# One PSUM bank per head, matmuls ordered by array shape, and GpSimd held behind VectorE in an attention and gated-MLP kernel

## The chip, the cores and the metric

The kernel runs on one core of a Trainium2 chip. The metric is the device time of one execution in microseconds (us), median of the runs shown; lower is better.

## What is computed

Eight batch entries, 12 heads, 448 positions, head size 64. Attention with RMS-normed q and k, then a gated MLP with a residual:

```python
q_n, k_n = (rmsnorm(q, g_q), rmsnorm(k, g_k))
scores = matmul(q_n, k_n.T) / sqrt(64)
attn = exp(scores - max); attn = attn / (sum(attn) + 1e-09)
x = heads side by side of matmul(attn, v)          # (8, 448, 768)
h = gelu_tanh(x @ w_in)                            # w_in (768, 1024)
u, v = h[..., :512], h[..., 512:]
v_n = (v - mean) / sqrt(var + 1e-06) * g_ln
v_s = einsum('ts,bsd->btd', w_sg, v_n) + b_sg      # over positions
out = x + (u * v_s) @ w_out                        # w_out (512, 768)
```

All inputs and the output are float32 (some inputs are handed to the device as 64-bit words and decoded there); most matmuls run on pairs of float16 parts, high and low.

## The kernel before

The kernel does not issue instructions as it is written. `tile_attn_gmlp_kernel` records every operation on a `Tape`, as tasks with a priority (its place in the program plus an offset). `Tape.schedule` then plays a list scheduler: each engine takes the ready task of lowest priority, each operation has a cost from `Tape.cost`, and START gives the delay between engines. `Tape.emit` issues everything in the planned order through one line (L425 of the profile), so nearly all rows of the profile carry this line and are told apart by their tiles. The engines run their queues in order, so the plan fixes what stands behind what.

The work is cut into 24 units of four heads. For each unit: squares and norms of q and k (`squares`, `norms`), the multiplications and the split into float16 halves (`split`: tiles qk and hl; by GpSimd, with VectorE and ScalarE), a transposing DMA into qt, then `scores`. There seven blocks t each give a pair of heads: 12 matmuls (tile s, in the 64x64 array shape, four at a time), on VectorE a minimum (tile jk, result nm), on ScalarE the exponential (tile ex), then its two halves (ahl) and a transposing DMA into at. `pv` makes the attention output in two parts per unit, 48 in all: the reciprocals of the sums in small steps on GpSimd and VectorE (rx, ry, rh, rl in `recips`), a factor row by TensorE (tile row, 128x64 shape), then 48 matmuls into tile pv. Of these 12 have 64 rows of contraction (64x64 shape) and 36 have 128 (128x64 shape). `moe` is the MLP of one batch entry: mv and mu (x @ w_in), a cluster of gelus, layernorm, ms (over positions), mo (residual and output), all but some of it in the 128x128 shape. `weights` decodes and splits the weights on VectorE and ScalarE (tiles dec, wi, wp, wr) during the first batches. MOFF is the offset that lets `moe` stand behind attention in priority.

A change of the array shape costs the planner SWITCH (133 or 92 ns), and it may put off a task of another shape while one of the present shape lies within HYST of it.

PSUM has eight banks. Before, four are a ring of two score tiles (pool ps_s, each tile both heads' banks), and four are given out by the plan to pv, row, psc and the MLP (pool ps_m, BANKS = 4, MOST: at most one pv tile and four of the MLP).

VectorE operations of some forms and all GpSimd operations are marked `port`: in the plan they do not overlap. Nothing enforces this when the kernel runs.

Of the kernel before, what the change touches and what calls it, by code (L numbers as in the profile page):

```python
# [24 lines left out]

MOFF, MOFF0, GP = 340, 100, 350

# [15 lines left out]

NS, BANKS, MOST = 2, 4, dict(pv=1, mm=4, mme=3)
NQK, NVR, RAWB = 2, 2, 3
# [7 lines left out]
BIAS = dict(A=0, V=0, G=0)  # L53
SLACK = (0, 0)
OVER, PATIENCE = dict(V=130, G=150), 300
START = dict(T=60, A=34, V=33, G=85, S=28, N=0)


class Tile:

    def __init__(self, pool, args, kw, tag, cap):
        self.pool, self.args, self.kw, self.tag, self.cap = pool, args, kw, tag, cap
        self.users, self.writes, self.reads, self.real, self.bank = [], [], [], None, None

# [32 lines left out]
class Tape:  # L97

    def __init__(self, tc):
        self.tc, self.tiles, self.tasks, self.off, self.count = tc, {}, [], 0, 0  # L100
        self.after = set()
        self.grouped = self.last = None
        self.masks, self.swap = {}, None

    def free(self, ap):
# [21 lines left out]
    def cost(self, q, op, a, kw):  # L127

        aps = [x for x in kw.values() if isinstance(x, bass.AP)]
        n = max([self.free(x) for x in aps], default=1)  # L130
        wide = [k for k in ("in_", "in0", "in1") if k in kw and self.free(kw[k]) > max(n // 2, 1)]
        psum = any(self.tiles[kw[k].tensor.name].pool.space for k in wide if kw[k].tensor.name in self.tiles)
        if q.eng == "T":
            t, big = kw["lhsT"], kw["rhs"]
            rows, cols = (64 if ap_n <= 64 else 128 for ap_n in (t.shape[0], self.free(t)))
            m = self.free(big)
            d = max(m / 2.4, 26.7 if cols == 64 else 53)
            if big.dtype == F32R:
                d = max(d, 186)
            if big.dtype == F32:  # L140
                d = max(4 * m / 2.4, 250)
            return d * rows * cols / 128 ** 2 + (4 if rows == cols == 128 else 3), 170, (rows, cols)
        if q.eng != "S" and "dma" in op:
            return 700, 4000, None
        if q.eng == "S":
            b = n * kw["out"].shape[0] * mybir.dt.size(kw["out"].dtype)
            if "transpose" in op:
                return 1530, b / 458752, True
            return 600, b / 220e3, False
        if "preload" in op:  # L150
            return 1283, 0, None
        if q.eng == "A":
            ptr = sum(isinstance(kw.get(k), bass.AP) for k in ("bias", "scale"))
            return 0.833 * n + (70 if psum else 100) + 80 * ptr + (200 if "accum_out" in kw else 0), 100, None
        if q.eng == "V":
            if op == "reciprocal":
                return 70 + 6.5 * n, 75, None
            ptr = sum(isinstance(kw.get(k), bass.AP) for k in ("scalar", "scalar1", "scalar2"))
            one = len(wide) == 1 and not psum and "reduce" not in op and "bn" not in op
            f32 = one and (mybir.dt.size(kw[wide[0]].dtype) == 4 or kw[wide[0]].dtype == U16)  # L160
            return (0.52 if f32 else 1.04) * n + 75 + 40 * ptr + (70 if "accum_out" in kw else 0), 75, None
        if n < 100:
            return 1.5 * n + 185, 20, None
        wide = [k for k in wide if len([x for x in kw[k].ap if x[0]]) == len(kw[k].ap)]
        return (1.86 if len(wide) > 1 else 2.5 if op == "tensor_scalar" else 1.64) * n + 210, 20, None

    def port(self, q, op, kw):

        if q.eng == "G":
            return True  # L170
        if q.eng != "V" or max(self.free(v) for v in kw.values() if isinstance(v, bass.AP)) < 16 or op not in ("tensor_tensor", "scalar_tensor_tensor", "tensor_scalar", "tensor_copy"):
# [21 lines left out]
    def record(self, q, op, a, kw):  # L193
# [5 lines left out]
        pe = q.eng == "T"  # L199
        if t is None or self.grouped is None and not (pe and t.eng == "T" and t.key == (outs[0].tensor.name, mode)  # L200
                                                      and t.off == self.off):
            t = Task(q.eng, self.count + self.off)
            t.id, t.off, t.key = len(self.tasks), self.off, (outs[0].tensor.name, mode) if pe else None
            self.tasks.append(t)
# [42 lines left out]
    def schedule(self):  # L247
# [16 lines left out]
        for tl in self.tiles.values():  # L264
            if not tl.users:
                continue
            if tl.pool.name == "ps_m":
                kind = tl.kw["tag"]
                free_order = tl.kw["name"] in ("psc", "sw_")
                tl.users[0].opens.append((tl, kind, None if free_order else last.get(kind[:2])))  # L270
                if not free_order:
# [35 lines left out]
        while left:  # L307
            moved = True
            let_go()
            while moved:  # L310
                moved = False
                for e in START:
# [71 lines left out]
                    for s in succ[t.id]:  # L384
                        f = T[s].eng
                        r = free[e] + 15 if f == e and not T[s].alts else end + START[f]
                        ready[s] = max(ready[s], r)
# [15 lines left out]
    def emit(self, real_pools):  # L403
        tc = self.tc

        def real(v):
# [8 lines left out]
            return bass.AP(tensor=r.tensor, offset=v.offset, ap=v.ap)  # L415

        for t in self.schedule():
            for c in t.calls:
# [5 lines left out]
                first = (kw.pop("out"),) if op == "memset" else ()  # L424
                getattr(q.nc_eng, op)(*first, *a, **kw)  # L425


@with_exitstack
def kernel(
# [39 lines left out]
    for n_, b_, s_ in (("const", 1, None), ("ld", 3, None), ("prep", 2, None), ("att", 2, None), ("sml", 4, None),  # L469
                       ("xp", NX, None), ("ps_s", NS, PS), ("ps_m", 1, PS)):  # L470
# [3 lines left out]
    const, ld, prep, att, sml, xp, ps_s, ps_m = made  # L474
    mlp = Pool(tape, "mlp", 1)
# [86 lines left out]
    def decode(dst, raw, most=None):  # L562
# [3 lines left out]
        V.tensor_scalar(out=di, in0=hi, scalar1=0x7FFFFFFF, scalar2=None, op0=ALU.bitwise_and)  # L566
        if most is None:
            V.tensor_scalar(out=dst, in0=dst, scalar1=LEAST, scalar2=None, op0=ALU.max)
        else:
            V.tensor_scalar(out=dst, in0=dst, scalar1=LEAST, scalar2=None, op0=ALU.max, op1=ALU.max, accum_out=most)  # L570
        V.tensor_scalar(out=di, in0=di, scalar1=3, scalar2=0x3FFFFFF8, op0=ALU.logical_shift_left, op1=ALU.bitwise_and)
# [221 lines left out]
    def scores(u):  # L793
# [5 lines left out]
        for t in range(C7):  # L799
            if t in (0, C4):  # L800
                at = att.tile([P, 2 * C7, (C4 - t // C4) * P], F16, name=f"at{t // C4}", bufs=1)
                U[u]["at"].append(at)
            ps = ps_s.tile([P, 2, 512], F32, name="s")
            for m, (qx, kx) in enumerate(((0, 2), (1, 2), (0, 3))):
                for h in range(2):
                    hs = slice(h * HP, (h + 1) * HP)
                    for j in range(NG):
                        mm(out=ps[j * HP:(j + 1) * HP, h, 0:S].rearrange("p (c n) -> p c n", n=HP),
                           lhsT=qt[hs, qx, t * P + j * HP:t * P + (j + 1) * HP],
                           rhs=kt[hs, kx, j], start=(m == 0), stop=(m == 2))  # L810
            nm = sml.tile([P, 2], F32, name="nm", bufs=6)
            for h in range(2):
                jk = att.tile([P, S], BF16, name="jk", bufs=2)
                V.tensor_scalar(out=jk, in0=ps[:, h, 0:S], scalar1=UP, scalar2=None, op0=ALU.add, op1=ALU.min,
                                accum_out=nm[:, h:h + 1])
            ex = att.tile([P, 2, S], I32, name="ex", bufs=NEX)
            for h in range(2):
                A.activation(out=ex[:, h], in_=ps[:, h, 0:S], func=AF.Exp, scale=-1.0, bias=nm[:, h:h + 1], accum_out=sums[:, t, h:h + 1])
            yield
# [35 lines left out]
    def pv(u, e):  # L855
# [259 lines left out]
    pend = None  # L1115
    wts = low(weights(), 0)
    load_qk(0, [SP, A] if EARLY else None)
# [116 lines left out]
```

## Time and profile before

| | |
|---|---|
| median of three runs | 884.81 us (882.46 to 885.58) |
| the profiled execution | 881.78 us, of which the span of instructions is 880.0 |
| TensorE busy | 766.3 us, 87% of the span |
| ScalarE busy | 727.9 us, 83% |
| VectorE busy | 685.8 us, 78% |
| GpSimd busy | 317.6 us, 36% |
| mean granted TensorE clock | 0.957 |

Engines are PE (TensorE), PEld (its weight loads), DVE (VectorE), ACT (ScalarE), POOL (GpSimd) and SP (which starts DMAs). The busy share of TensorE is a mean over stages that differ; matmul ends are modelled, so times between starts say more than durations. Times in the rows are us from the span's start.

### The profile page before, as it was taken

To read this page: it belongs to the slowest core of one execution; us is meant where nothing else is said; L and a number is where in the kernel's file an instruction comes from. 1 tells how busy PE (TensorE), PEld (TensorE's weight loads), DVE (VectorE), ACT (ScalarE), POOL (GpSimd) and SP (SyncE) were. 2 spreads that over 40 slices of the span, in tenths; PEclk is the share of its full clock that TensorE was granted. 3 is DMA by queue.
4 is the path that set the end of the run, shared out by engine and by line. 5 is a ranking of instruction groups with operands and counts; after the bars stand their busy time and mean duration, and the time that the engine had idled before them with its cause. 6 is when DMAs were issued, how large, how long until landed. Compare 5 with 4: busy or idle time off the path is not lost.

```text
span 880.0 us, 20978 instructions
## 1 busy us (share of the span) xinstructions
PE 766.3 (87%) x7766; PEld 456.0 (52%) x7766; DVE 685.8 (78%) x1690; ACT 727.9 (83%) x1495; POOL 317.6 (36%) x458
## 2 busy tenths in 40 slices
PE   0445669547999999999999999999999999999997
PEld 0222334223574467544754477456745575457457
DVE  6899997998887987868877979688887978583150
ACT  4779789987988998989999989799999978884351
POOL 3554520274453344535433506542553341000000
PEclk9997869856999999999999999999999999999999
DMA  6999989889899959998999599969999698635002
GB/s 161 262 256 233 227 178 216 162 187 215 167 221 227 204 116 217 231 199 167 188 221 219 129 215 188 226 157 180 210 226 175 124 183 178 147 85 100 19 1 72
DMA packets 433942, 155.96 MB, mean 177 GB/s; under 512 B 402544, under 2 KB 427696, under 8 KB 433840
## 3 DMA queue, kind: packets, MB, share of 16 engines
q1 hardware_dynamic: 433840, 154.63, 85.8%
q8 instruction: 61, 1.00, 0.5%
q14 instruction: 41, 0.34, 0.1%
HBM read 43.57 MB, written 11.01 MB: 62 GB/s over the span
## 4 chain that ended last, share of the span: by engine, by line
PE 56%; DVE 18%; ACT 14%; issue 5%; DMA 3%; POOL 2%; SPq 0%; ACTq 0%; DVEq 0%; POOLq 0%
PE pv L425 11%; PE s L425 8%; DVE jk L425 4%; ACT ex L425 3%; DVE dec L425 3%; ACT ahl L425 3%; ACT L425 2%; PE row L425 2%; DMA at<-ahl 2%; DVE vl L425 1%; DVE ahl L425 1%; DVE ss L425 1%; ACT u L425 1%; POOL qk L425 1%; ACT sqk L425 1%
## 5 line engine op out<-in xcount | busy, mean ns | idle before, releaser
L425 ACT ACTIVATE ex<-s,nm 128x448 int32<-128x448 f32 x336 | 212.3, 634 | 29.8 <-DVE jk L425 25.3
L425 DVE TENSOR_SCALAR_CACHE_REDUCE jk<-s 128x448 bf16<-128x448 f32 x336 | 199.5, 617 | 43.5 <-PE s L425 42.6
L425 PE MATMUL s<-qt 64*64 64x448 f16 x2016 | 148.3, 383 | 79.7 <-ACT ex L425 58.1
L425 ACT ACTIVATE ahl<-ex 128x896 f16<-128x896 uint16 x191 | 179.7, 952 | 8.5 <-DMA at<-ahl 7.8
L425 PEld LDWEIGHTS <-vh 128*64 128x64 f16 (+2 forms) x1792 | 100.5, 111 | 89.7 <-issue 64.0
L425 PE MATMUL pv<-at,vh 128*64 128x256 f16 (+3 forms) x1536 | 140.8, 274 | 5.7 <-DMA at<-ahl 3.1
L425 PEld LDWEIGHTS <-qt 64*64 64x64 f16 x2016 | 62.5, 111 | 117.9 <-issue 76.7
L425 DVE TENSOR_SCALAR ahl<-ex 128x896 f16<-128x896 uint16 x145 | 103.7, 716 | 25.0 <-ACT ex L425 20.7
L425 POOL TENSOR_TENSOR hl<-qk,hl 128x896 f16<-128x896 f32 (+2 forms) x69 | 97.2, 1419 | 21.1 <-DVE hl L425 13.4
L425 POOL TENSOR_SCALAR rx<-sums 128x8 f32<-128x8 f32 (+1 forms) x48 | 16.5, 344 | 213.6 <-ACT ex L425 212.2
L425 POOL TENSOR_TENSOR qk<-qk,ny 128x896 f32<-128x896 f32 x47 | 83.1, 1787 | 1.8
L425 PEld LDWEIGHTS <-wi 128*128 128x128 f16 x576 | 52.0, 98 | 53.0 <-issue 7.7
L425 PE MATMUL pv<-at,vl 128*64 128x192 f16 (+3 forms) x768 | 74.4, 274 | 0.0
L425 PEld LDWEIGHTS <-vl 128*64 128x64 f16 (+2 forms) x896 | 49.3, 110 | 45.0 <-issue 27.7
L425 PEld LDWEIGHTS <-xh 128*128 128x128 f16 (+1 forms) x648 | 48.8, 103 | 42.9 <-issue 18.8
L425 POOL TENSOR_TENSOR qk<-qk,gg 128x896 f32<-128x896 f32 x23 | 48.4, 2106 | 60.3 <-ACT sqk L425 57.2
L425 ACT ACTIVATION_READ_ACCUMULATOR ex<-s,nm 128x1 f32 x336 | 69.0, 205 | 0.0
L425 DVE TENSOR_TENSOR pv<-pv,row 128x512 f32<-128x512 f32 (+1 forms) x48 | 30.2, 629 | 39.5 <-PE pv L425 39.3
L425 DVE TENSOR_REDUCE ss<-sqk 128x14 f32<-128x896 f32 x48 | 51.7, 1079 | 9.2 <-ACT sqk L425 9.1
L425 ACT ACTIVATE sqk<-qk 128x896 f32<-128x896 f32 x48 | 45.7, 954 | 2.9 <-DMA qk<-in_k_dram 1.5
L425 PEld LDWEIGHTS <-xl 128*128 128x128 f16 (+1 forms) x408 | 36.6, 103 | 20.4 <-issue 1.7
L425 ACT ACT_TABLE_LOAD x36 | 46.2, 1283 | 0.6
(1104 smaller groups left out, 1797.7 us busy)
## 6 DMA issues: line engine op xcount, KB each, us to landing
qk<-in_q_dram SPq DMA_DIRECT2D x48, 224.0 KB, 3.8
qk<-in_k_dram SPq DMA_DIRECT2D x48, 224.0 KB, 4.6
out_dram<-ot SPq DMA_DIRECT2D x56, 192.0 KB, 3.2
raw<-in_moe_w_in_dram SPq DMA_DIRECT2D x12, 512.0 KB, 5.3
vr<-in_v_dram SPq DMA_DIRECT2D x32, 192.0 KB, 3.6
vr<-in_v_dram SPq DMA_DIRECT2D x32, 144.0 KB, 3.6
rawo<-in_moe_w_out_dram SPq DMA_DIRECT2D x8, 384.0 KB, 4.0
at<-ahl SPq DMA_TRANSPOSE x168, 4.2
```

Of the source, the lines that this page charges most:

```text
L425: getattr(q.nc_eng, op)(*first, *a, **kw)
```

## The change

Four things change together.

- All eight PSUM banks go to pool ps_m and are given out by the plan. A score block has a tile, and so a bank, for each head. `mate` makes both heads' matmuls one task. `opens` lets a task start when as many banks are free as it needs and the kind's limit (MOST: pv 2, MLP 4, scores 6) allows it.
- `pv` goes through its matmuls by shape: the six 64-row blocks of both head pairs first, then the 128-row blocks, with cuts after blocks 5 and 14 (CUTS).
- `emit` adds a wait: a GpSimd operation marked `port` with a cost over LONG (500) waits for the last VectorE operation marked `port` that the plan put before it.
- The costs in `Tape.cost` are altered by some tens of ns, operations with accum_out are no longer marked `port`, MOFF goes from 340 to 300. WOFF = 0, AGAIN (15, and 85 for GpSimd) is new for a task that follows on its own engine.

```diff
-MOFF, MOFF0, GP = 340, 100, 350
+MOFF, MOFF0, GP = 300, 100, 350
-NS, BANKS, MOST = 2, 4, dict(pv=1, mm=4, mme=3)
+BANKS, MOST = 8, dict(pv=2, mm=4, mme=3, sc=6)
+LONG = 500
+CUTS = (5,14)
+AGAIN = dict(T=15, A=15, V=15, G=AG, S=15, N=15)
...
+        key = (self.tiles[outs[0].tensor.name].mate or outs[0].tensor.name, mode) if pe else None
...
         def opens(t, now):
-            return all((before is None or before.bank is not None) and min(bank_free) <= now
-                       and (held["pv"] if kind == "pv" else held["mm"] + held["mme"]) < MOST[kind]
-                       for _, kind, before in t.opens)
+            n = len(t.opens)
+            kind = t.opens[0][1] if n else None
+            return not n or (all(x is None or x.bank is not None for _, _, x in t.opens)
+                             and sum(x <= now for x in bank_free) >= n
+                             and (held["mm"] + held["mme"] if kind[:2] == "mm" else held[kind]) + n <= MOST[kind])
...
-                getattr(q.nc_eng, op)(*first, *a, **kw)
+                ins = getattr(q.nc_eng, op)(*first, *a, **kw)
+                if t.port and q.eng == "V":
+                    holder = ins
+                elif t.port and holder is not None and t.occ > LONG:
+                    tc.add_manual_dep(ins.ins, holder.ins.name, self.behind, reason="shared port")
...
-            ps = ps_s.tile([P, 2, 512], F32, name="s")
+            ps = [ps_m.tile([P, 512], F32, name="s", tag="sc") for h in range(2)]
+            for x in ps:
+                tape.tiles[x.tensor.name].mate = ps[0].tensor.name
...
-        for j in range(NG):
-            r = R[NG * u + j]
-            for k_, (v_, o, hx) in enumerate(blocks):
-                for h, (ks, c) in enumerate(hx):
-                    mm(out=pc[h * HP:(h + 1) * HP, j], lhsT=r[v_][ks, c], rhs=av[ks, o + c, j, 0:n],
-                       start=(j == 0 and k_ == 0), stop=(j == NG - 1 and k_ == len(blocks) - 1), skip_group_check=True)
-                if k_ == 5:
-                    yield
-            if j == 0:
+        steps = [(j, x) for part in (blocks[:3], blocks[3:]) for j in range(NG) for x in part]
+        for k_, (j, (v_, o, hx)) in enumerate(steps):
+            for h, (ks, c) in enumerate(hx):
+                mm(out=pc[h * HP:(h + 1) * HP, j], lhsT=R[NG * u + j][v_][ks, c], rhs=av[ks, o + c, j, 0:n],
+                   start=(k_ == 0), stop=(k_ == len(steps) - 1), skip_group_check=True)
+            if k_ in CUTS:
                 yield
```

In the order of TensorE's instructions the first place is one attention-output tile in the middle of the run. Before, this is the end of its first run of six in the 64x64 shape (vh and vl are the halves of v of one head pair, at1 the transposed exponentials, mu the MLP, wi its weight):

```order
L425 LDWEIGHTS vl_6449
L425 MATMUL pv_7276<-at1_6907,vl_6449 64x3x64
L425 LDWEIGHTS vh_6425
L425 MATMUL pv_7276<-at1_6907,vh_6425 64x3x64
L425 LDWEIGHTS vh_6425
L425 MATMUL pv_7276<-at1_6907,vh_6425 64x3x64
L425 LDWEIGHTS wi_779
L425 MATMUL mu__7263<-xh_6016,wi_779 128x448
```

It goes on in further runs of 6, 12, 6, 6 and 12 matmuls, with six of mu between (and a single other one, before the last), six runs in all. In the change the same kind of tile has the second head pair's blocks (vh_6647, vl_6677) straight behind the first's:

```order
L439 LDWEIGHTS vh_6548
L439 MATMUL pv_7272<-at1_7033,vh_6548 64x3x64
L439 LDWEIGHTS vh_6647
L439 MATMUL pv_7272<-at1_7033,vh_6647 64x3x64
L439 LDWEIGHTS vh_6647
L439 MATMUL pv_7272<-at1_7033,vh_6647 64x3x64
L439 LDWEIGHTS vl_6677
L439 MATMUL pv_7272<-at1_7033,vl_6677 64x3x64
```

Its runs are now 12, 18 and 18: three in place of six. Counted over the whole order, the array shape changes 606 times before and 363 times in the change; behind the first 1542 matmuls it is 485 and 280.

The second place is GpSimd's queue, at one unit's split, with the semaphores that each instruction waits for (DVE is VectorE's). Before:

```order
L425 TENSOR_TENSOR qk<-qk,ny 128x896 [waits DMAHW7_49,DMAHW0_49,Pool_49]
L425 TENSOR_TENSOR qk<-qk,ny 128x896
L425 TENSOR_TENSOR hl<-qk,hl 128x2x7x64 [waits DMAHW0_49,Activation_49]
L425 TENSOR_TENSOR hl<-qk,hl 128x2x4x64 [waits DMAHW6_49,Activation_49]
L425 TENSOR_TENSOR hl<-qk,hl 128x2x3x64 [waits Activation_49]
```

In the change:

```order
L439 TENSOR_TENSOR qk<-qk,ny 128x896 [waits DMAHW0_49,DMAHW7_49,DVE_49,Pool_49]
L439 TENSOR_TENSOR qk<-qk,ny 128x896 [waits DVE_49]
L439 TENSOR_TENSOR hl<-qk,hl 128x2x7x64 [waits DMAHW6_49,Activation_49]
L439 TENSOR_TENSOR hl<-qk,hl 128x2x4x64 [waits DMAHW0_49,DVE_49,Activation_49]
L439 TENSOR_TENSOR hl<-qk,hl 128x2x3x64 [waits DVE_49,Activation_49]
```

The operations and their order are the same; four of the five now wait for VectorE. Over the whole queue, 31 of 139 such long operations waited for VectorE before, and 98 of 138 do in the change. Beside this, one multiply (qk), one scaling (ahl) and one cast (hl) are on another engine than before.

## Rows read from the trace of the kernel before

**Rows 1.** Busy time in stretches: length, PE, PEld, DVE, ACT, POOL (instructions), clock, DMA.

```profile
0.00:50.00 50.00, 10.95 (x102) 5.55 (x103) 38.81 (x81) 29.41 (x55) 21.78 (x38) 1.00 0.91 213
50.00:100.00 50.00, 32.28 (x354) 17.07 (x353) 48.62 (x111) 44.64 (x90) 23.80 (x26) 0.86 1.12 244
100.00:150.00 50.00, 36.62 (x393) 19.69 (x390) 45.39 (x132) 42.84 (x85) 12.44 (x19) 0.80 1.01 195
150.00:200.00 50.00, 27.94 (x275) 15.04 (x274) 45.87 (x107) 46.57 (x98) 22.12 (x34) 0.74 0.87 187
200.00:250.00 50.00, 44.00 (x418) 27.12 (x421) 43.88 (x101) 43.61 (x88) 20.54 (x25) 0.85 0.99 192
250.00:300.00 50.00, 50.00 (x554) 27.29 (x554) 42.90 (x100) 43.37 (x94) 26.65 (x40) 1.00 1.08 223
...
400.00:500.00 100.00, 97.60 (x1004) 56.23 (x998) 82.83 (x201) 93.16 (x193) 47.95 (x63) 1.00 0.90 185
...
600.00:700.00 100.00, 97.88 (x1040) 57.08 (x1038) 83.27 (x205) 93.54 (x199) 41.49 (x59) 1.00 0.96 189
```

**Rows 2.** Waits of TensorE from 0 to 250 us: total us, times, longest.

```profile
PE s L425 <- ACT ex L425: 53.4, 21, 7.9
```

**Rows 3.** Waits of TensorE from 200 to 870 us.

```profile
PE s L425 <- ACT ex L425: 7.0, 9, 1.4
```

**Rows 4.** TensorE in order of time, 428 to 433 us: start, us, operation, shape, count.

```profile
428.46 0.52 PE L425 MATMUL pv<-at,vh 128*64 128x256 f16 x6
428.91 0.44 PE L425 MATMUL mo__6402<-wo_h,gh 128*128 128x384 f32 x1
429.19 0.34 PE L425 MATMUL mo__6402<-wo_l,gh 128*128 128x384 f32 x1
...
431.17 0.34 PE L425 MATMUL mo__6476<-wo_l,gh 128*128 128x384 f32 x1
431.34 0.34 PE L425 MATMUL mo__6476<-wo_h,gl 128*128 128x384 f32 x1
431.61 0.52 PE L425 MATMUL pv<-at,vl 128*64 128x256 f16 x6
431.96 0.49 PE L425 MATMUL pv<-at,vh 128*64 128x256 f16 x6
432.38 0.76 PE L425 MATMUL s<-qt 64*64 64x448 f16 x12
```

**Rows 5.** The chain that ended last, 80 to 120 us: start, us, what.

```profile
83.91 1.06 DVE hsv L425
...
86.82 2.26 DVE dec L425
...
97.23 2.13 DVE dec L425
...
113.33 1.77 DVE wi_up L425
```

**Rows 6.** VectorE in order of time, 84 to 104 us.

```profile
86.37 0.41 DVE L425 TENSOR_SCALAR dec<-dec 128x512 int32<-128x512 int32 x1
86.82 2.26 DVE L425 SCALAR_TENSOR_TENSOR dec<-raw,dec 128x512 int32<-128x512 int32 x1
...
97.15 2.22 DVE L425 TENSOR_SCALAR dec<-dec 128x512 int32<-128x512 int32 x1
...
100.83 0.68 DVE L425 SCALAR_TENSOR_TENSOR dec<-raw,dec 128x512 int32<-128x512 int32 x1
```

**Rows 7.** GpSimd in order of time, 84 to 104 us.

```profile
86.53 3.57 POOL L425 TENSOR_TENSOR hl<-qk,hl 128x896 f16<-128x896 f32 x2 [1.57 <-ACT hl L425]
...
97.00 2.08 POOL L425 TENSOR_TENSOR qk<-qk,gg 128x896 f32<-128x896 f32 x1 [2.67 <-ACT sqk L425]
```

**Rows 8.** Waits over the whole run: total us, times, longest.

```profile
POOL rx L425 <- ACT ex L425: 212.2, 31, 16.4
...
POOL hl L425 <- DVE hl L425: 13.4, 15, 1.8
...
PEld L425 <- POOL rh L425: 5.6, 5, 1.9
```

More of the change, by code (lines that the diff above doesn't have):

```diff
@@ L54 @@
 SLACK = (0, 0)
+LONG = 500
+WOFF = 0
+CUTS = (5,14)
+CA = 200
+CV = 70
+AG = 85
 OVER, PATIENCE = dict(V=130, G=150), 300
 START = dict(T=60, A=34, V=33, G=85, S=28, N=0)
+AGAIN = dict(T=15, A=15, V=15, G=AG, S=15, N=15)
 class Tile:
@@ L62, in __init__ @@
         self.pool, self.args, self.kw, self.tag, self.cap = pool, args, kw, tag, cap
-        self.users, self.writes, self.reads, self.real, self.bank = [], [], [], None, None
+        self.users, self.writes, self.reads, self.real, self.bank, self.mate = [], [], [], None, None, None
 class Pool:
@@ L103, in __init__ @@
         self.masks, self.swap = {}, None
+        self.behind = mybir.DependencyInfo(mybir.DependencyClass.Sync, mybir.DependencyReason.SCHED_ONLY)
     def free(self, ap):
@@ L153, in cost @@
             ptr = sum(isinstance(kw.get(k), bass.AP) for k in ("bias", "scale"))
-            return 0.833 * n + (70 if psum else 100) + 80 * ptr + (200 if "accum_out" in kw else 0), 100, None
+            return 0.833 * n + (52 if psum else 95) + 85 * ptr + (CA if "accum_out" in kw else 0), 100, None
         if q.eng == "V":
@@ L158, in cost @@
             ptr = sum(isinstance(kw.get(k), bass.AP) for k in ("scalar", "scalar1", "scalar2"))
-            one = len(wide) == 1 and not psum and "reduce" not in op and "bn" not in op
+            one = len(wide) == 1 and not psum and "reduce" not in op and "bn" not in op and "accum_out" not in kw
             f32 = one and (mybir.dt.size(kw[wide[0]].dtype) == 4 or kw[wide[0]].dtype == U16)
-            return (0.52 if f32 else 1.04) * n + 75 + 40 * ptr + (70 if "accum_out" in kw else 0), 75, None
+            return (0.52 if f32 else 1.04) * n + 70 + 50 * ptr + (CV if "accum_out" in kw else 0), 85, None
         if n < 100:
@@ L170, in port @@
             return True
-        if q.eng != "V" or max(self.free(v) for v in kw.values() if isinstance(v, bass.AP)) < 16 or op not in ("tensor_tensor", "scalar_tensor_tensor", "tensor_scalar", "tensor_copy"):
+        if q.eng != "V" or "accum_out" in kw or max(self.free(v) for v in kw.values() if isinstance(v, bass.AP)) < 16 or op not in ("tensor_tensor", "scalar_tensor_tensor", "tensor_scalar", "tensor_copy"):
             return False
@@ L199, in record @@
         pe = q.eng == "T"
-        if t is None or self.grouped is None and not (pe and t.eng == "T" and t.key == (outs[0].tensor.name, mode)
-                                                      and t.off == self.off):
+        key = (self.tiles[outs[0].tensor.name].mate or outs[0].tensor.name, mode) if pe else None
+        if t is None or self.grouped is None and not (pe and t.eng == "T" and t.key == key and t.off == self.off):
             t = Task(q.eng, self.count + self.off)
-            t.id, t.off, t.key = len(self.tasks), self.off, (outs[0].tensor.name, mode) if pe else None
+            t.id, t.off, t.key = len(self.tasks), self.off, key
             self.tasks.append(t)
@@ L269, in schedule @@
                 free_order = tl.kw["name"] in ("psc", "sw_")
-                tl.users[0].opens.append((tl, kind, None if free_order else last.get(kind[:2])))
+                before = last.get(kind[:2])
+                if free_order or any(x is before for x, _, _ in tl.users[0].opens):
+                    before = None
+                tl.users[0].opens.append((tl, kind, before))
                 if not free_order:
@@ L385, in schedule @@
                         f = T[s].eng
-                        r = free[e] + 15 if f == e and not T[s].alts else end + START[f]
+                        r = free[e] + AGAIN[e] if f == e and not T[s].alts else end + START[f]
                         ready[s] = max(ready[s], r)
@@ L566, in decode @@
         V.tensor_scalar(out=di, in0=hi, scalar1=0x7FFFFFFF, scalar2=None, op0=ALU.bitwise_and)
[L567 to L570, printed above, removed]
+        more = {} if most is None else dict(op1=ALU.max, accum_out=most)
+        V.tensor_scalar(out=dst, in0=dst, scalar1=LEAST, scalar2=None, op0=ALU.max, **more)
         V.tensor_scalar(out=di, in0=di, scalar1=3, scalar2=0x3FFFFFF8, op0=ALU.logical_shift_left, op1=ALU.bitwise_and)
@@ L807, in scores @@
                     for j in range(NG):
-                        mm(out=ps[j * HP:(j + 1) * HP, h, 0:S].rearrange("p (c n) -> p c n", n=HP),
+                        mm(out=ps[h][j * HP:(j + 1) * HP, 0:S].rearrange("p (c n) -> p c n", n=HP),
                            lhsT=qt[hs, qx, t * P + j * HP:t * P + (j + 1) * HP],
@@ L817, in scores @@
             for h in range(2):
-                A.activation(out=ex[:, h], in_=ps[:, h, 0:S], func=AF.Exp, scale=-1.0, bias=nm[:, h:h + 1], accum_out=sums[:, t, h:h + 1])
+                A.activation(out=ex[:, h], in_=ps[h][:, 0:S], func=AF.Exp, scale=-1.0, bias=nm[:, h:h + 1], accum_out=sums[:, t, h:h + 1])
             yield
```

9 lines of the change are left out of this document (5 added, 4 removed).

## Prediction

> **What bounds the kernel now.** I first cut the span into stretches and read how busy each engine is [rows 1]. There are two regimes. Up to 250 us TensorE is far from full (10.95, 32.28, 36.62, 27.94 and 44.00 of 50 us) while VectorE is at 48.62, 45.39, 45.87 and 43.88 of 50 from 50 us on. From 250 us TensorE is full: 50.00 of 50, then 97.60 and 97.88 of 100, and its clock is granted at 1.00, the 2.4 GHz level. ScalarE is close behind it there, at 93.16 and 93.54 of 100.
>
> The waits say the same. Of TensorE's waits before 250 us the largest is scores waiting for the exponentials, 53.4 us [rows 2]; from 200 to 870 us that same wait is 7.0 us [rows 3]. So a saving in TensorE's own stream is worth its full size after 250 us and nothing before it. A saving before 250 us has to come from VectorE, or from ScalarE.
>
> The third view is TensorE's order of time in the full stretch [rows 4]. Equal matmuls of the output projection start 0.17 us apart (431.17, 431.34). The next group has another array shape and starts 0.27 us later (431.61): 0.10 us that no matmul uses. Six attention-output matmuls in the 128x64 shape take 0.35 us (431.61 to 431.96); the same six followed by a 64x64 group take 0.42 (431.96 to 432.38), and followed by a 128x128 group 0.45 (428.46 to 428.91): 0.07 and 0.10 more. After the last of these the first projection matmul holds the engine for 0.28 us (428.91 to 429.19) where its like takes 0.17. I take 0.10 us for one change of shape; the bounds are 0.07 and 0.10 + 0.11 = 0.21.
>
> The fourth view is the chain that ended last between 80 and 118 us [rows 5], nearly all VectorE. Four of its pieces are single instructions of 1.06 to 2.26 us. VectorE's order of time [rows 6] shows what their like takes: 0.68 where the chain's took 2.26, 0.41 where one took 2.22. In GpSimd's order of time [rows 7] a long operation began just ahead: two from 86.53 ahead of VectorE's 86.82, one of 2.08 from 97.00 ahead of VectorE's 97.15. VectorE starts, and stands until GpSimd lets go.
>
> **The change, part by part.**
>
> *Fewer changes of shape.* The attention output is ordered by shape, with both heads' score matmuls still one task, and the planner lays out TensorE's order anew. I counted the changes of shape in both orders: 606 before, 363 now. The windows up to 250 us hold 102 + 354 + 393 + 275 + 418 = 1542 matmuls [rows 1]; behind that many, 485 changes are left before and 280 now. So 205 go in the full stretch: 205 x 0.10 = 20.5 us, with bounds 205 x 0.07 = 14 and 205 x 0.21 = 43. The other 38 lie where TensorE waits anyway and are worth nothing; what hides them is the 53.4 us of [rows 2], and without it they would be 3.8. Between the ends I stay at 20.5 for TensorE's own stream, since only a return to the projection shows the extra 0.11.
>
> I do not take all of it. ScalarE has the same work to do in about 3.4% less time (20.5 of 600 us): 93.5 would become 96.8, fuller than any stretch here shows. Those stretches are about half of the full part, so I let a third of the saving be lost in them: 20.5 x (1 - 1/6) = 17 us.
>
> *A bank for each head, all eight given out.* No matmul is added. A score pair's first bank comes free one exponential earlier, and three pairs can be in flight instead of two. In the full stretch that could save at most the 7.0 us of [rows 3], but a score pair still needs two free banks and ScalarE's pace stays. I take 0. It can also cost: the MLP and the attention output had four banks to themselves and now find two when three pairs are open (a rival, below).
>
> *GpSimd waits.* Long GpSimd operations with a VectorE wait go from 31 of 139 to 98 of 138 in the orders. The nearest row for such a wait is GpSimd's wait for VectorE's halves, 13.4 us in 15 times, 0.9 us each [rows 8]; 67 x 0.9 = 60 us more of waiting. It is covered: GpSimd already stands 212.2 us waiting for exponentials ahead of the reciprocals [rows 8]. Queued behind a waiting operation are the reciprocals' small steps, and TensorE waits for those (5.6 us in all [rows 8]). I cost it at 0; without the cover it is the slower rival.
>
> What it can give is VectorE's stalls in the first 250 us. The four pieces of [rows 5] exceed their like by 1.58 and 1.72 (the two with a twin in [rows 6]), and by at least 1.36 and 0.65 for the two on a handful of elements, which cannot need more than the 0.41 of a 512-wide one: 5.3 us in 38 us of chain. The rest of the first 250 us is less purely VectorE, so I take 5.3 for this piece and as much again for all the others, and two thirds of the 10.6 as removed: 7 us. The bounds are 0 and 5.3 x 250 / 38 = 35. After 250 us the same stalls are covered by TensorE.
>
> The page "SBUF — State Buffer" of the Trainium skill, section "SBUF: two separate sides", says that the pair of ports the two engines share is locked by whichever starts first, for its whole instruction, and that the other fully blocks. The stalls in [rows 5] to [rows 7] agree. Followed to its end the rule speaks against this part: the new wait settles only who comes first, GpSimd still holds the pair as long, and the next VectorE operation may meet the lock instead; this term would then be 0 in place of 7.
>
> *The rest.* MOFF from 340 to 300, the corrected costs and the count of engine choices (one cast, one scaling and one multiply change engine) only move work; each engine's count of operations stays within one or two. At 0.6 to 1.0 us each, off TensorE, I take 0. The queue of DMA starts has the same transfers.
>
> **Sum.** 881.8 (the profiled execution) - 17 - 7 = 857.8. The median of the three runs stands 3.0 above that execution, so the same loss off the median gives **861 us**.
>
> **The rivals.**
>
> *The lock only changes hands.* VectorE's stalls are as many as before, at other instructions. For it: GpSimd's long operations stay 1.7 to 2.1 us and as many. Against: a stall like 86.82 comes from GpSimd being early, which the wait forbids. Result: 884.8 - 17 = 868.
>
> *ScalarE becomes the bound.* For it: 93.16 and 93.54 [rows 1]. Against: other stretches leave it room, and some of its work may go to VectorE. Then half of 20.5 is realised: 884.8 - 10 - 7 = 868. The page "TensorEngine Tiling (Array Packing)" of the Trainium skill, section "PSUM Bottleneck", warns of this: a faster TensorE leaves the emptying of PSUM as it was. No stretch before shows ScalarE above 93.54, so the trace has not reached that point.
>
> *More than that.* The third score pair also shortens the 53.4 us of [rows 2] and the lock's stalls go altogether: 20.5 + 10.6 and, of the 53.4, some 8: 884.8 - 39 = 846.
>
> *No change.* The rows' 0.10 is paid again as waits for banks, since scores may hold six of eight, and the first 250 us stay as they are: 884.8 less 0 to 4. Against it: scores waited only 7.0 us after 200 with four banks.
>
> *Slower.* GpSimd's long operations wait for a VectorE that is behind its plan, and the reciprocals' steps queue behind them, so the factor row and the attention output on TensorE come late. There are 48 such groups; 0.9 us each is 43 us: 884.8 - 24 + 43 = 904. It decides from 24 / 48 = 0.5 us a group. For it: GpSimd runs in order and its steps alternate with the long ones. Against: GpSimd waits 212.2 us for the exponentials there, so it is early.
>
> **How the numbers follow.** My forecast of 861 gets 0.45, the lock that changes hands 0.13, ScalarE as the bound 0.13, the larger gain 0.14, no change 0.08, slower 0.07. A measurement of this kernel can tell about 0.5% from no change, which is 880.4 to 889.2 here. Faster by more: 0.45 + 0.13 + 0.13 + 0.14 = 0.85; within: 0.08; slower: 0.07. The range goes from 845, at the larger gain, to 879, above both cases at 868 and the lower bound of the shape term alone (884.8 - 14 = 871); it leaves out half of the larger gain and the two cases at the end, about 0.2.
>
> **What would show it.** Right: shape changes still near 0.10 us each and TensorE at or above 97 of 100 after some 240 us; the stage before it shorter by several us; 2 us single instructions gone from the VectorE chain; GpSimd's waits for VectorE larger by tens of us with no line of TensorE waiting for it. Wrong: scores or attention output waiting for ScalarE beyond 15 us after 250 (ScalarE or the banks are the bound), the long VectorE instructions still there (the lock), or TensorE's row waiting for GpSimd by more than 20 us (the slower case).

## The result, and the profile after

The changed kernel takes **861.22 us** (median of six runs, 859.08 to 864.01), the kernel before, run beside it, 883.08 (881.17 to 885.58). The ratio is 0.9754 [0.9728, 0.9779], and 861 had been forecast. The profiled execution takes 860.37 us, its span is 858.6; 880.0 before.

The first view is the busy time in stretches, columns as in [rows 1].

```profile
50.00:100.00 50.00, 26.29 (x282) 17.33 (x284) 42.82 (x98) 41.27 (x82) 23.02 (x26) 0.67 1.11 225
200.00:250.00 50.00, 43.02 (x477) 29.56 (x478) 44.81 (x110) 45.09 (x96) 24.00 (x33) 0.88 1.01 193
250.00:300.00 50.00, 49.97 (x534) 28.50 (x530) 42.84 (x102) 46.46 (x102) 26.13 (x37) 1.00 1.14 225
300.00:400.00 100.00, 95.18 (x1037) 62.69 (x1032) 79.61 (x205) 89.38 (x187) 39.84 (x57) 0.98 1.02 203
400.00:500.00 100.00, 97.79 (x1055) 59.97 (x1054) 81.18 (x206) 94.42 (x200) 36.95 (x59) 1.00 0.99 187
600.00:700.00 100.00, 98.03 (x1092) 65.23 (x1085) 85.24 (x223) 94.92 (x205) 43.30 (x64) 1.00 1.01 199
```

From 300 to 400 us, which [rows 1] leaves out, the kernel before shows:

```profile
300.00:400.00 100.00, 97.32 (x1029) 59.32 (x1032) 80.93 (x208) 89.90 (x193) 40.45 (x59) 1.00 0.98 192
```

From 400 us TensorE is as full as before and gets more done: 1055 and 1092 matmuls in windows that held 1004 and 1040. From 300 to 400 us it is less full (95.18 in place of 97.32) and its granted clock is 0.98 in place of 1.00; the last section comes back to that. ScalarE rises to 94.42 and 94.92. Before 250 us the picture is mixed: from 50 to 100 us there are only 282 matmuls (354 before) at a granted clock of 0.67 (0.86), from 200 to 250 us 477 (418).

To see where the 21.4 us of the span came from, both spans are cut where 1544 matmuls are done. The same view, before:

```profile
0.00:250.40 250.40, 152.20 (x1544) 84.73 (x1548) 222.97 (x529) 207.47 (x412) 101.08 (x140) 0.85 0.98 206
250.40:880.00 629.60, 614.09 (x6230) 371.29 (x6222) 462.85 (x1162) 520.43 (x1084) 216.55 (x319) 1.00 0.82 166
```

and after:

```profile
0.00:248.20 248.20, 148.79 (x1544) 89.26 (x1544) 212.57 (x525) 201.05 (x400) 95.25 (x138) 0.79 0.96 201
248.20:858.60 610.40, 594.21 (x6230) 385.88 (x6222) 455.58 (x1167) 521.27 (x1097) 209.27 (x319) 1.00 0.88 174
```

The full stretch is 19.2 us shorter, the first stage 2.2. In the full stretch (the second line of each view) 6230 matmuls keep TensorE busy for 614.09 before and 594.21 now: 19.9 us less. What is left of the stretch is time in which TensorE does nothing (called holes below): 629.60 - 614.09 = 15.5 before, 16.2 now.

TensorE's order of time in the full stretch answers to [rows 4]:

```profile
430.53 0.34 PE L439 MATMUL mo__6579<-wo_h,gl 128*128 128x384 f32 x1
430.80 0.52 PE L439 MATMUL pv<-at,vh 128*64 128x256 f16 x6
431.15 0.49 PE L439 MATMUL pv<-at,vl 128*64 128x256 f16 x6
431.48 0.49 PE L439 MATMUL pv<-at,vh 128*64 128x256 f16 x6
431.80 0.22 PE L439 MATMUL row<-ident_h,rh 128*64 128x128 f16 x2
...
432.24 1.90 PE L439 MATMUL s<-qt 64*64 64x448 f16 x36
```

One step between shapes is still 0.27 us (430.53 to 430.80), but 18 attention-output matmuls and the factor row now stand in one shape, and 36 score matmuls in another.

TensorE's waits, 0 to 250 us (total us, times, longest), answer to [rows 2]:

```profile
PE s L439 <- DMA qt<-hl: 21.3, 1, 21.3
PE s L439 <- ACT ex L439: 15.8, 7, 6.0
PE pv L439 <- ACT ex L439: 12.2, 1, 12.2
PE row L439 <- POOL rh L439: 11.9, 1, 11.9
```

and from 200 to 870 us to [rows 3]:

```profile
PE row L439 <- POOL rh L439: 11.9, 1, 11.9
PE ms__4409 L439 <- DVE xl L439: 4.8, 1, 4.8
...
PE s L439 <- ACT ex L439: 0.6, 1, 0.6
```

Scores waiting for exponentials fall from 53.4 to 15.8 us in the first stage and from 7.0 to 0.6 later. That is much less waiting in the first stage, and yet the stage is only 2.2 us shorter. The chain that ended last names what stood there instead (start, us, what):

```profile
65.63 7.83 DMA at<-ahl
73.60 2.75 PE pv L439 x30
...
89.70 5.29 DMA at<-ahl
95.12 5.13 PE pv L439 x48
...
104.00 2.15 DVE dec L439 x5
```

From 65 to 100 us it now runs mostly through the transposing DMAs and the attention output behind them, where [rows 5] had one long VectorE instruction after another; the VectorE pieces left in it from 80 to 120 us are at most 1.25 us for a single instruction. VectorE's order of time, next to [rows 6]:

```profile
86.49 1.62 DVE L439 TENSOR_TENSOR hsv<-v_v,wi_v 128x1 f32<-128x1 f32 x1
88.57 2.24 DVE L439 SCALAR_TENSOR_TENSOR dec<-raw,dec 128x512 int32<-128x512 int32 x2
90.73 1.47 DVE L439 TENSOR_SCALAR dec<-raw 128x512 int32<-128x512 int32 x2
...
94.24 0.68 DVE L439 SCALAR_TENSOR_TENSOR dec<-raw,dec 128x512 int32<-128x512 int32 x1
...
96.33 2.30 DVE L439 SCALAR_TENSOR_TENSOR dec<-raw,dec 128x512 int32<-128x512 int32 x2
```

and GpSimd's, next to [rows 7]:

```profile
86.21 1.88 POOL L439 TENSOR_TENSOR hl<-qk,hl 128x896 f16<-128x896 f32 x1
88.78 2.80 POOL L439 TENSOR_TENSOR hl<-qk,hl 128x512 f16<-128x512 f32 x2 [0.68 <-ACT hl L439]
...
95.39 2.09 POOL L439 TENSOR_TENSOR qk<-qk,gg 128x896 f32<-128x896 f32 x1 [1.95 <-DVE dec L439]
```

GpSimd now waits where it used to start early (1.95 us for VectorE's dec at 95.39). Two dec instructions take 2.24 and 2.30 us where 2 x 0.68 would be usual, so some 0.9 us of stall is left in each pair, against 1.58 and 1.72 in one instruction before. But the pair at 90.73 takes 1.47 us where 2 x 0.41 would be usual: part of the first stall now stands there. VectorE still runs into a GpSimd operation now and then: hsv, on one element a partition, starts at 86.49 behind GpSimd's hl of 86.21 and ends with it, at 88.1.

### The profile page after: what moved, and what is told of

The parts are those of the page before. It is cut to its first block, busy times and chain, and to the rows that moved or that the text cites. A ratio compares the mean times of both kernels' runs of the same rounds, so it can differ in the third digit from the quotient of the medians.

```text
span 858.6 us, 21024 instructions
## 1 busy us (share of the span) xinstructions
PE 743.0 (87%) x7766; PEld 475.1 (55%) x7766; DVE 668.2 (78%) x1691; ACT 722.3 (84%) x1495; POOL 304.5 (35%) x457
## 4 chain that ended last, share of the span: by engine, by line
PE 55%; ACT 17%; DVE 12%; DMA 9%; issue 5%; POOL 1%; SPq 1%; ACTq 0%; DVEq 0%; POOLq 0%
PE pv L439 11%; PE s L439 7%; DMA at<-ahl 6%; ACT ex L439 4%; ACT ahl L439 3%; DVE jk L439 2%; ACT L439 2%; ACT sqk L439 2%; PE row L439 1%; DVE ahl L439 1%; DMA qk<-in_k_dram 1%; ACT vg L439 1%; ACT u L439 1%; ACT vh L439 1%; DVE pv L439 1%
## 5 line engine op out<-in xcount | busy, mean ns | idle before, releaser
L439 ACT ACTIVATE ahl<-ex 128x896 f16<-128x896 uint16 x192 | 181.9, 957 | 9.5 <-DMA at<-ahl 8.9
L439 PE MATMUL s<-qt 64*64 64x448 f16 x2016 | 142.8, 375 | 48.4 <-DMA qt<-hl 21.3
L439 PEld LDWEIGHTS <-vh 128*64 128x64 f16 (+2 forms) x1792 | 103.2, 112 | 103.6 <-issue 55.7
L439 PE MATMUL pv<-at,vh 128*64 128x192 f16 (+3 forms) x1536 | 133.0, 275 | 27.6 <-ACT ex L439 12.3
L439 POOL TENSOR_TENSOR hl<-qk,hl 128x896 f16<-128x896 f32 (+2 forms) x69 | 93.7, 1364 | 41.7 <-ACT hl L439 9.7
L439 PEld LDWEIGHTS <-wi 128*128 128x128 f16 x576 | 54.5, 99 | 55.5 <-issue 7.2
L439 POOL TENSOR_TENSOR qk<-qk,ny 128x896 f32<-128x896 f32 x46 | 77.1, 1690 | 14.5 <-DVE ahl L439 7.5
L439 PEld LDWEIGHTS <-xh 128*128 128x128 f16 (+1 forms) x648 | 49.7, 102 | 47.7 <-issue 20.8
L439 ACT ACTIVATION_READ_ACCUMULATOR ex<-s,nm 128x1 f32 x336 | 71.6, 213 | 0.0
L439 PEld LDWEIGHTS <-vl 128*64 128x64 f16 (+2 forms) x896 | 56.1, 114 | 12.8 <-issue 0.7
L439 DVE TENSOR_REDUCE ss<-sqk 128x14 f32<-128x896 f32 x48 | 51.8, 1079 | 10.2 <-ACT sqk L439 10.1
L439 ACT ACTIVATE xh<-pv 128x512 f16<-128x512 f32 (+1 forms) x48 | 26.2, 547 | 24.4 <-DVE pv L439 23.7
```

Of the source, the lines that this page charges most:

```text
L439: ins = getattr(q.nc_eng, op)(*first, *a, **kw)
```

## The experiments

The span of a kernel is compared with that of the change by the same cut: the first stage until about 1542 matmuls are done, then the full stretch. Holes are that stretch less TensorE's busy time. "Behind" counts the shape changes in the planned order behind 1542 matmuls, 485 before and 280 in the change. The kernel before took 883.08 to 883.77 us beside all these runs; two kernels less than some 2 us apart are not told apart. Each cut of a span is of one profiled execution, so a difference of 1 or 2 us in one stage is a hint and no more.

### Do the waits do anything? (two kernels)

The change without its waits, in the same order:

```diff
-LONG = 500
+LONG = 1e9
```

> The changed kernel without GpSimd's new waits: the order on every engine is the changed kernel's, only the 67 added waits are gone. As predicted (the waits take VectorE's stalls off the first 250 us, worth 7 us): 861 + 7 = 868 us. Rival, the lock only changes hands: 861, within 2. Between them, from the traces of both kernels: before has 1542 matmuls behind it at 250 us, the change 1575, which is some 2 to 3 us: 863 to 864. VectorE instructions near 2 us should be back in the first 250 us in the first and third case.

Measured: 865.96 us (before beside it 883.77), ratio 0.9804 [0.9784, 0.9825]. The waits are worth 4.7 us in the change.

The kernel before with the waits alone; its order stays as it was:

```diff
+LONG = 500
...
-                getattr(q.nc_eng, op)(*first, *a, **kw)
+                ins = getattr(q.nc_eng, op)(*first, *a, **kw)
+                if t.port and q.eng == "V":
+                    holder = ins
+                elif t.port and holder is not None and t.occ > LONG:
+                    tc.add_manual_dep(ins.ins, holder.ins.name, self.behind, reason="shared port")
```

> The kernel before with nothing but the GpSimd waits added, its order unchanged. As predicted: 883 - 7 = 876 us. The lock only changes hands: 883, within 2. Slower rival (steps of the reciprocals come late behind the long operations): above 888, with TensorE's row waiting for GpSimd by more than 20 us.

Measured: 877.55, ratio 0.9933 [0.9913, 0.9953], 6.2 us. The windows, first of the kernel without waits, both stages:

```profile
0.00:249.40 249.40, 148.97 (x1542) 89.34 (x1544) 219.09 (x529) 201.40 (x401) 98.94 (x138) 0.79 0.94 200
249.40:861.90 612.50, 594.66 (x6230) 386.22 (x6222) 458.45 (x1164) 520.96 (x1095) 214.06 (x319) 0.99 0.88 173
```

then of the kernel with the waits alone, its full stretch:

```profile
248.50:875.50 627.00, 614.16 (x6230) 371.00 (x6222) 457.19 (x1162) 520.63 (x1084) 213.73 (x319) 1.00 0.83 166
```

With TensorE's order unchanged and its busy time within half a microsecond (594.66 and 594.21; 614.16 and 614.09) the stretch after 250 us gets 2.1 and 2.6 us shorter in the two profiled pairs, mostly in its holes. VectorE's busy time shows the stalls that went: 219.09 to 212.57 in the first stage, 458.45 to 455.58 after it. At one place of VectorE's order of time without waits a stall is whole again, against 0.68 for the same instruction in the change (94.24 above):

```profile
92.93 2.46 DVE L439 SCALAR_TENSOR_TENSOR dec<-raw,dec 128x512 int32<-128x512 int32 x1
```

The stalls around it mostly moved. Without the waits the pair now at 88.57 takes 2.96 us, the one at 90.73 takes 0.75 and the one at 96.33 takes 1.31. In the change the first stall is shared by two pairs (2.24 and 1.47, the same 3.71 in sum), and about half of the stall at 92.93 stands in the pair at 96.33 (2.30).

### What does a change of shape cost?

The change, with the matmuls of each attention-output tile dealt out again among its own places in the plan, so that the shapes alternate as before; everything else stays in its order. 491 behind:

```diff
...
+            few = [c for c in calls if self.cost(c[0], c[1], c[2], c[3])[2] == (64, 64)]
+            many = [c for c in calls if c not in few]
+            mixed = few[:4] + many[:8] + many[8:14] + few[4:8] + many[14:22] + many[22:28] + few[8:] + many[28:]
...
```

> The changed kernel with the attention output's 48 matmuls dealt out anew inside their own places: each run gets four 64-row ones among its 128-row ones. No other task moves, banks and waits stay. The array shape changes 626 times in place of 363, 491 in place of 280 behind the first 1542 matmuls. If a change of shape costs TensorE 0.10 us in the full stretch, as the prediction's first term has it: 861 + 211 x 0.10 = 882 us. If the gain came from the banks, the order or the first 250 us, and a change of shape is hidden: 861 to 864.

Measured: 883.18 (883.77 before), ratio 0.9992 [0.9979, 1.0005]. Divided by the 211 changes of shape in the full stretch, the 22.0 us are **0.104 us each**, and they give the whole gain back. The full stretch:

```profile
250.30:883.60 633.30, 619.74 (x6234) 374.62 (x6222) 452.05 (x1164) 523.63 (x1095) 209.15 (x319) 0.99 0.85 167
```

Its holes are 13.6 us: what came is busy time of TensorE. In this one execution the account by stages is rougher than the quotient: busy time is 25.5 us more, 0.121 for each change, at a granted clock of 0.99; holes are 2.6 less; and the first stage, with 52 more changes, is 2.1 longer. So the price is about 0.1 us, without a third figure.

### One part alone, or one part undone

Shape order alone, the new loop of `pv` in the kernel before; 334 behind:

```diff
-        for j in range(NG):
...
+        steps = [(j, x) for part in (blocks[:3], blocks[3:]) for j in range(NG) for x in part]
```

> The kernel before with only the attention output by shape; the banks, costs and waits as before. 334 changes of shape behind the first 1542 matmuls in place of 485: 884 - 151 x 0.104 = 868 us. If the shapes only pay together with the eight banks: 876 or more.

Measured: 868.10 (883.68), ratio 0.9822 [0.9805, 0.9839]: 15.6 us for 151 changes of shape, 0.103 each. In its full stretch TensorE's busy time is 15.3 us less than before, 0.101 for each, and the holes are 2.8 more:

```profile
249.30:866.40 617.10, 598.84 (x6230) 382.08 (x6222) 459.47 (x1168) 520.83 (x1087) 214.54 (x317) 1.00 0.86 170
```

The old loop in the change (the same diff turned round); 378 behind:

> The changed kernel with the attention output written as before (one head pair after the other), planned anew: 485 changes of shape, 378 behind the first 1542 matmuls (280 in the change). By the price of a change of shape: 861 + 98 x 0.10 = 871 us. If the order inside the attention output does not matter: 861, within 2. If it is all of the gain: 882.

Measured: 868.32 (883.77), ratio 0.9829 [0.9812, 0.9846]: 7.1 us given back for 98 changes, which at 0.104 would be 10.2.

The banks alone, in the kernel before (old loop, old costs and MOFF, no waits; the new AGAIN is in it); 397 behind:

```diff
-NS, BANKS, MOST = 2, 4, dict(pv=1, mm=4, mme=3)
+BANKS, MOST = 8, dict(pv=2, mm=4, mme=3, sc=6)
...
-            ps = ps_s.tile([P, 2, 512], F32, name="s")
+            ps = [ps_m.tile([P, 512], F32, name="s", tag="sc") for h in range(2)]
```

> The kernel before with only the PSUM part: a bank for each head, all eight given out by the plan (limits pv 2, MLP 4, scores 6). Attention output, costs and MOFF as before, no added waits. Planned anew it has 397 changes of shape behind the first 1542 matmuls in place of 485. By the price that e3 gave (22.0 us for 211, 0.104 each) and nothing else: 884 - 88 x 0.104 = 875 us. If the deeper scores also cost the 6 us by which the change is behind in the first 100 us: 881. If they give more, by fewer waits for exponentials: below 872.

Measured: 869.63 (883.68), ratio 0.9844 [0.9824, 0.9863]. The banks alone gain 14.1 us, of which 88 changes of shape explain 9.2. Its windows to 248 us show where more of it is:

```profile
0.00:248.00 248.00, 152.26 (x1550) 86.52 (x1550) 222.35 (x535) 202.35 (x406) 102.65 (x139) 0.83 1.01 209
```

1550 matmuls are done by 248.00 us, where the kernel before needs 250.40 for 1544.

The banks undone in the change (the diff turned round; one pv tile at most); 338 behind:

> The changed kernel with the PSUM part undone: two score tiles of two banks each in a ring, four banks given out, at most one attention-output tile. Waits, shape order, costs and MOFF as changed. 338 changes of shape behind the first 1542 matmuls. By their price alone: 861 + 58 x 0.104 = 867 us. If the eight banks also cost the late start seen in the first 100 us: 861 to 863. If the banks are worth more than the shapes they save (e5 came out 5 us below its price): 871 or more.

Measured: 861.66 (883.25), ratio 0.9753 [0.9725, 0.9781]: the same as the change. Its windows:

```profile
0.00:246.10 246.10, 147.92 (x1542) 89.62 (x1546) 217.83 (x534) 202.70 (x405) 97.65 (x140) 0.84 0.99 209
246.10:858.50 612.40, 598.40 (x6230) 379.65 (x6228) 452.38 (x1163) 518.95 (x1086) 212.55 (x317) 1.00 0.86 171
```

Beside the change, TensorE is busy 4.2 us longer (58 changes of shape more), with 2.2 us less of holes and a first stage 2.1 us shorter: the two sides cancel.

### The costs and MOFF

The change with the old `cost`, the old rule for `port` and MOFF = 340:

> The changed kernel with the planner's costs, its rule for the shared port and MOFF as before. 278 changes of shape behind the first 1542 matmuls (280 in the change). If these numbers only move work, as predicted: 861, within 2. If they are what makes up for the late start of the MLP in the first 100 us: 866 or more. If they cause that late start: 855 to 858.

Measured: 869.27 (883.68), ratio 0.9843 [0.9828, 0.9857]: 8 us back, at 278 behind. So one of the three matters, and not by the number of shapes. Two kernels take it apart, the old `cost` alone:

```diff
-            return 0.833 * n + (52 if psum else 95) + 85 * ptr + (CA if "accum_out" in kw else 0), 100, None
+            return 0.833 * n + (70 if psum else 100) + 80 * ptr + (200 if "accum_out" in kw else 0), 100, None
...
```

> The changed kernel with only the durations in the planner's cost function as before; the port rule and MOFF stay changed. 283 changes of shape behind the first 1542 matmuls. If the durations are what e7 lost (8 us): 868 to 870. If MOFF or the port rule is: 861, within 2.

and the old MOFF alone (301 behind):

```diff
-MOFF, MOFF0, GP = 300, 100, 350
+MOFF, MOFF0, GP = 340, 100, 350
```

> The changed kernel with only MOFF back at 340. 301 changes of shape behind the first 1542 matmuls in place of 280. By their price alone: 861 + 21 x 0.104 = 863 us. If MOFF is what e7 lost: 868 to 870.

Measured: the old costs 861.16 (883.25), ratio 0.9748 [0.9713, 0.9783], no difference; the old MOFF 871.05, ratio 0.9856 [0.9823, 0.9889], 9.8 us given back. The old `port` rule by itself was not tried, nor the old `AGAIN`. The full stretch with the old MOFF, and two windows of it:

```profile
245.80:869.60 623.80, 600.74 (x6230) 386.05 (x6222) 463.45 (x1178) 517.16 (x1082) 218.14 (x319) 0.99 0.88 170
```

```profile
300.00:400.00 100.00, 94.26 (x1013) 60.25 (x1009) 79.68 (x207) 87.29 (x185) 42.65 (x56) 0.98 1.03 199
400.00:500.00 100.00, 93.54 (x1016) 57.99 (x1015) 78.58 (x197) 90.87 (x189) 40.95 (x58) 0.98 1.01 188
```

Busy time is 6.5 us more and the holes are 23.1 us, 6.9 more; the first stage is 2.4 shorter. From 300 to 400 us TensorE is at 94 of 100 with a clock granted at 0.98, and so nearly is the change (95.18, 0.98); from 400 to 500 the change has 97.79 and 1.00 where this kernel stays at 94 and 0.98. 21 changes of shape explain 2.2 us of the busy time.

### Can fewer changes of shape still gain?

The planner may put a task off for longer to stay in a shape (252 behind):

```diff
-SWITCH, HYST = (133, 92), 160
+SWITCH, HYST = (133, 92), 450
```

> The changed kernel with HYST 450 in place of 160, so that the planner puts off a change of shape longer: 252 changes behind the first 1542 matmuls in place of 280. By the price alone: 861 - 28 x 0.104 = 858 us. If what is put off comes late for ScalarE and VectorE (ScalarE as the bound): 861 or more.

Measured: 904.91 (883.68), ratio 1.0244 [1.0221, 1.0267]. The slowest of all has the fewest changes of shape:

```profile
250.20:901.10 650.90, 603.20 (x6230) 389.34 (x6226) 450.60 (x1163) 526.71 (x1100) 210.79 (x319) 0.97 0.79 161
```

Holes of 47.7 us in place of 16.2, and a granted clock of 0.97, with 603.20 us of busy time in place of 594.21 for as many matmuls.

One cut in an attention output, so two runs in place of three (261 behind):

```diff
-CUTS = (5,14)
+CUTS = (5,)
```

> A try at a faster kernel: the change with one cut in the attention output in place of two, so runs of 12 and 36 matmuls. 261 changes of shape behind the first 1542 matmuls in place of 280. By their price alone: 861 - 19 x 0.104 = 859 us. If the longer run keeps scores waiting, as in e8: 865 or more.

Measured: 868.29 (883.25), ratio 0.9844 [0.98, 0.9887]. Against the change:

```profile
251.40:866.90 615.50, 591.66 (x6232) 384.11 (x6228) 463.52 (x1172) 517.28 (x1081) 211.28 (x319) 1.00 0.86 169
```

Busy time falls by 2.5 us, close to 19 x 0.104 = 2.0; the holes grow to 23.8, by 7.6, and the first stage is 3.2 longer. No kernel of the twelve is measurably faster than the change.

## Why the prediction was right, point by point

**What bounds.** Right: the full stretch is TensorE's, and its length is its busy time plus the holes of the plan. One of its windows misses the 97 of 100 that was named as a sign: 95.18 from 300 to 400 us, where one wait for VectorE's xl takes 4.8 us; the kernel before has no such wait. Six kernels with a granted clock of 1.00 in it line up: 614.1 us of busy time at 485 changes of shape (before, and with the waits alone), 598.8 at 334, 598.4 at 338, 594.2 at 280, 591.7 at 261. From the first to the last that is 22.4 / 224 = 0.100 us each.

**Fewer changes of shape: 17 of 20.5.** The mechanism and the price of about 0.10 are shown from both sides, by dealing the shapes back (0.104) and by the new loop alone (0.103). The 0.11 in the upper bound does not belong to it: before, the first projection matmul behind bf16 ones holds TensorE for 0.26 us (420.76 to 421.02) without any change of shape. Without the waits the full stretch gains 629.6 - 612.5 = 17.1, which is the number taken, but the reason given for the deduction failed. ScalarE does rise to 94.92, and TensorE hardly waits for it: scores wait 0.6 us for exponentials from 200 us on. The 3.4 us that are missing from 20.5 are 1.1 of busy time and 2.3 of holes (17.8 against 15.5). The page "TensorEngine Tiling (Array Packing)" of the Trainium skill, section "PSUM Bottleneck", was cited for the rival. No run here shows what it warns of: the highest ScalarE window of 100 us in the full stretch, 95.96 from 400 to 500 us with the old costs, belongs to a kernel as fast as the change (861.16).

**Banks: 0.** Right as a sum, and not as the reasons given. The banks save shape changes, because more score blocks can stand side by side (36 score matmuls in one run), and they cost a slower start and some holes; undoing them leaves 861.66. In the first stage TensorE runs 62 score matmuls at its first start; this is TensorE's order of time of the change:

```profile
21.26 4.87 PE L439 MATMUL s<-qt 64*64 64x448 f16 x62 [21.26 <-DMA qt<-hl]
...
57.44 0.42 PE L439 MATMUL pv<-at,vh 64*64 64x256 f16 x2 [12.15 <-ACT ex L439]
...
73.60 0.36 PE L439 MATMUL pv<-at,vh 64*64 64x192 f16 x2 [4.73 <-DMA at<-ahl]
...
76.28 1.33 PE L439 MATMUL s<-qt 64*64 64x448 f16 x12
...
79.12 0.66 PE L439 MATMUL mv__853<-wi,xh 128*128 128x512 f16 x2
```

The first 24 were followed by a wait before; now the first attention output comes at 57.44 (55.43 before) after 12.15 us of waiting and the first full MLP run at 79.12 (72.87 before). With the banks undone these are 54.15 and 69.72. The granted clock is lower too: after the pause ahead of 73.60, twelve score matmuls take 1.33 us, which at 1.00 take 0.76 [rows 4]. With the banks undone, 342 matmuls fall between 50 and 100 us at a clock of 0.83, against 282 at 0.67:

```profile
50.00:100.00 50.00, 30.26 (x342) 18.11 (x341) 49.40 (x118) 41.69 (x86) 20.66 (x25) 0.83 1.15 236
```

It is the banks in this plan and not the banks as such: alone in the kernel before, they leave the first full MLP run at 70.57.

**The waits: 7 us, all in the first 250 us.** The size was a little high (4.7 in the change, 6.2 alone). The step that failed, as far as two profiled pairs show it, is "After 250 us the same stalls are covered by TensorE": of the 3.3 us between the two profiled spans 2.1 lie after it, and of 4.5 with the waits alone 2.6. That a stalled VectorE there delays things that TensorE's queue comes to fits the holes; no single case was traced. That GpSimd's longer waiting costs nothing held: its waits for VectorE sum to 201.4 us with the waits and 174.6 without, 27 more (60 had been forecast), and the kernel is faster. TensorE's row does wait 11.9 us for GpSimd once, between 200 and 250 us, under the 20 us named as a sign of the slower case. That wait is not the work of the change's waits: without them it is 13.0.

**The lock changes hands.** Refuted as a zero (4.7 us), and not as a mechanism. The page "SBUF — State Buffer" of the Trainium skill, section "SBUF: two separate sides", has the shared ports locked by whichever of the two engines starts first, for those VectorE operations that use them. The rows agree that stalls move to other instructions (86.49, 90.73 and 96.33 above). What the waits gain is the part that does not come back: VectorE's busy time is 9.4 us less over the whole run (677.54 without, 668.15 with them), of which 4.7 show in the time.

**The first stage several us shorter.** Wrong: 2.2 us. The waits give 1.2 of it (249.4 to 248.2), and with the banks undone the stage is 246.1, so in this plan the banks' start costs about as much as the stage gained. That is not all: with the new banks and MOFF at 340 the stage is 245.8 as well. Why it stays at 248.2 in the change is open.

**The rest: 0.** Wrong for MOFF, which is worth 9.8 us in this plan, and right for the table of costs (861.16). Why MOFF = 340 leaves 7 us more of holes was only located, not shown: most of what is lost lies from 400 to 600 us (1016 and 1012 matmuls, in the change 1055 and 1068). It is a property of one plan and no fixed price: the new loop alone, with MOFF at 340, gets all of its 15.6.

**The parts don't add.** Taken back one at a time, shapes (22.0), waits (4.7), MOFF (9.8) and banks (0.4) make 36.9 us, and together they gave 21.9. Every variant but the waits and the dealt-back shapes makes the planner lay out a new order with holes of its own: from 2.2 us less than the change's (banks undone) to 7.6 more (one cut), and 31.5 more where tasks are put off. The count of shape changes doesn't tell them. The forecast of 861 was therefore nearer than its steps. The two that leave the order alone add up: everything but the waits gives 17.8 us (883.77 to 865.96; 17 forecast) and the waits 4.7 (7 forecast). Inside the 17.8 the misses on MOFF, the banks and the first stage cancelled, which is luck. So is the last step: 23.8 us had been taken off 884.8 and 21.9 came off 883.08, a base 1.7 lower.

## What to carry to other kernels

Where TensorE is full, count what its order makes it pay between matmuls of unlike shape, and price it from starts of neighbours in the trace; here the price read from a few starts (0.10) came out about the same when 151 changes were taken out (0.103) and 211 put back (0.104). With a planner and queues that run in order, judge a new order by TensorE's busy time and by its holes apart: fewer changes of shape bought with postponed tasks lost 44 us here. To learn what a part is worth, keep the order and take away that part alone, since everything that makes a new plan brings other holes along.

## What had not been expected of the hardware

Holes in a full TensorE can cost more than their own length. The change shows it once, in the 4.8 us that TensorE waits for xl and the 3 us after 308 us:

```profile
302.90:307.70 4.80, 0.04 (x3) 0.02 (x2) 3.29 (x7) 4.77 (x8) 0.00 (x0) 1.00 0.93 210
308.00:311.00 3.00, 3.00 (x10) 1.21 (x8) 1.64 (x2) 3.00 (x8) 0.96 (x1) 0.50 1.21 238
```

TensorE is busy again, and its granted clock is 0.50, the 1.2 GHz level: matmuls of ms start 0.37 us apart (308.55, 308.92), and 0.19 apart a little later (311.64, 311.83). Where tasks are put off (HYST 450) the mean granted clock of the full stretch is 0.97, so part of it ran at the 1.2 GHz level, and TensorE is busy for 603.2 us; by 0.10 us for each of 28 changes of shape fewer, it would be 594.2 - 2.8 = 591.4. Those 11.8 us come on top of 31.5 us more of holes. With MOFF at 340 it is the same on a smaller scale: a clock of 0.99, and 600.7 us where 21 changes more would make 596.3. Not every hole does it: with one cut the holes are 23.8 us, as many as with MOFF at 340, the clock is 1.00, and the 591.7 us of busy time are what 19 changes fewer would make (592.3) or less. Which holes are followed by the lower clock was not tested.
